# One row for each side's output: 320 columns copied by ScalarE, 256 by VectorE, stored as one run

## The chip, the core and the metric

The kernel runs on one core of one Trainium2 chip. The time is device microseconds of one execution, as the median of several runs. The profile is of one further execution, taken by the hardware profiler; positions inside it are in microseconds from the start of its span.

## What is computed

Two attention layers decode one token each, side A with a window of the last 2048 positions of its cache and side B with all 8192, and their outputs stand side by side in one row of 1152 bf16 values. For each side:

```python
q = (x @ wq).reshape(1, 1, 32, 128)             # x: 1 x 576, wq: 576 x 4096
k, v = k_cache, v_cache                         # 16 heads x 8192 x 128; side A: last 2048 rows
p = softmax(q . k * 128 ** -0.5)                # 32 query heads, two to a kv head
o = p . v                                       # 1 x 4096
return o @ wo                                   # wo: 4096 x 576
```

Everything is bf16 with fp32 accumulation, and the result is `concatenate([a, b])`.

## The kernel before

Every engine's program is a list, filled in order by `op` and `load` and emitted by the class `Prog` with one semaphore for each engine and one for each transfer in flight. An entry waits for the names in its `deps` and then runs in the order of its list.

All loads go through SP's queue into one ring buffer: wq of both sides, then K and V of four units of A and eight units of B, at last wo of A in one piece (`wo0.0`) and wo of B in six pieces (`wo1.0` to `wo1.5`, of 16, 8, 4, 2, 1 and 1 of the 32 slices, after the list `NWO`). The two x rows are loaded by ACT's queue into `xrow`, which lies in one partition.

The unit loop transposes K slabs on VectorE (L367), forms scores on TensorE (L384), takes exponentials on ScalarE (L433), multiplies with V (L460) and folds the result (L476). After the last unit a short chain (L515 to L532) normalizes both sides and leaves `oP`, 128 x 2 x 32.

Then comes the stretch that the change touches, the output projection into the PSUM tile `fb`, which is `qb[0]`. For each side P and each of 32 slices k it does two matmuls (L543) with a stationary operand of one column, `oP[:, P, k]`. They sum into two PSUM rows, 32 x (2P + n), of which row n = 0 holds the first columns of the side's output and row n = 1 the others. So A uses PSUM partitions 0 and 32, B partitions 64 and 96. The matmuls of one piece of wo are one entry, `F0.0` or `F1.0` to `F1.5`, and wait for that piece. When a side's last matmul is done, ScalarE copies row n = 0 to SBUF (`f0.0`, `f1.0`, L551) and VectorE row n = 1 (`f0.1`, `f1.1`, L554), both casting to bf16. SP stores the side when both are done (`out0`, `out1`, L555), and its program ends with a wait for `out1` (L561).

In the profile the copies and the store of both sides have the same lines.

Of the kernel before, what the change touches and what calls it, by code (L numbers as in the profile page):

```python
# [4 lines left out]
BF16 = mybir.dt.bfloat16  # L5
# [3 lines left out]
ACT = mybir.ActivationFunctionType  # L9
# [5 lines left out]
DM = 576  # L15
# [12 lines left out]
ZW = 128 + W0  # L28
ZA = 128 + 24
BIG = 1e30  # L30
RING = 72 * 1024
NSEM = 24
NKT = 3
# [3 lines left out]
class Prog:  # L37
# [9 lines left out]
    def op(self, eng, fn, deps=(), name=None):  # L47
        self.ops[eng].append((fn, tuple(deps), name, None))
        if name is not None:
            assert name not in self.where, name  # L50
            self.where[name] = (eng, len(self.ops[eng]) - 1)

    def load(self, eng, fn, sem, value, deps=(), name=None):
        self.ops[eng].append((fn, tuple(deps), None, sem))
        if name is not None:
            assert name not in self.dma, name
            self.dma[name] = (sem, value)
# [54 lines left out]
def bass_concat_heads__sliding_block_cached__gqa_block_cached__decode_kernel(nc, A_x, A_k_cache, A_v_cache, A_wq, A_wo,  # L112
# [6 lines left out]

    ring = nc.alloc_sbuf_tensor("ring", [128, RING], BF16)  # L120
    ktb = nc.alloc_sbuf_tensor("ktb", [128, NKT * SLAB], BF16)
# [36 lines left out]
    oq = nc.alloc_sbuf_tensor("oq", [128, 2, HQ], BF16)  # L158
    oP = nc.alloc_sbuf_tensor("oP", [128, 2, HQ], BF16)
    warm = nc.alloc_sbuf_tensor("warm", [128, 8], F32)  # L160
    outsb = nc.alloc_sbuf_tensor("outsb", [128, 288], BF16)

    sb = [nc.alloc_psum_tensor("sb%d" % b, [128, 512], F32) for b in range(2)]
    qb = [nc.alloc_psum_tensor("qb%d" % b, [128, 512], F32) for b in range(2)]
# [4 lines left out]
    def view(t, free, offset, dims, parts=128, p0=0):  # L169
        return bass.AP(tensor=t, offset=p0 * free + offset, ap=[[free, parts], *dims])  # L170

    pg = Prog(nc)
    op, load = pg.op, pg.load
    s_x = [nc.alloc_semaphore("s_x%d" % i) for i in range(2)]
    s_ld = [nc.alloc_semaphore("s_ld%d" % i) for i in range(NSEM)]
    s_out = nc.alloc_semaphore("s_out")
# [4 lines left out]
    def place(size, uses, issue, name):  # L181
        if at[0] + size > RING:
            at[0] = 0
        lo, hi = at[0], at[0] + size
        at[0] = hi
        deps = []
        for r in list(live):
            if r[0] < hi and lo < r[1]:
                deps += r[2]
                live.remove(r)  # L190
        n = nload[0]
        nload[0] += 1
        if n >= NSEM:
            deps += uses_of[n - NSEM]
        uses_of.append(list(uses))
        live.append((lo, hi, list(uses)))
        t = ring[:, lo:hi]
        load("sp", lambda e: issue(e, t), s_ld[n % NSEM], 16 * (n // NSEM + 1), deps=deps, name=name)
        return t
# [41 lines left out]
    wo_at = {}  # L241
    for P in range(2):
        k0 = 0
# [6 lines left out]
    def slab(kind, side, u, s):  # L250
# [7 lines left out]
       deps=["id0"], name="ident")  # L258
# [7 lines left out]
    for c in range(2):  # L266
        op("dve", lambda e, c=c: e.tensor_reduce(par[:, c:c + 1], view(identf, 128, c, [[2, 64]]), AX.X, ALU.add),
           deps=["identf"], name="par%d" % c)
# [3 lines left out]
    for P in range(2):  # L272
        op("dve", lambda e, P=P: e.tensor_copy(
            view(xdup, 256, 128 * P, [[2, 64], [1, 2]], parts=1),
            view(xrow, 2 * DM, P * DM + 512, [[1, 64], [0, 2]], parts=1)), deps=["x%d" % P], name="xd%d" % P)
        for k in range(5):
            def mm(e, P=P, k=k):
                if k < 4:
                    lhsT = view(xrow, 2 * DM, P * DM + k, [[4, 128]], parts=1)
                else:  # L280
                    lhsT = xdup[0:1, P, :]
                return e.matmul(banks[2 * P + k // 4][:, (k % 4) * 128:(k % 4 + 1) * 128], lhsT=lhsT,
                                rhs=onesb[0:1, :], start=True, stop=True)
            op("pe", mm, deps=["x%d" % P, "onesb", "xd%d" % P], name="xT%d.%d" % (P, k))
        op("dve", lambda e, P=P: e.tensor_copy(
            xrep[:, P, 0:4, :].rearrange("p k m -> p (k m)"), banks[2 * P][:, :]), deps=["xT%d.3" % P], name="xr%d.0" % P)
        for c in range(2):
            op("dve", lambda e, P=P, c=c: e.tensor_scalar(
                xrep[:, P, 4 + c, :], banks[2 * P + 1][:, 0:128], par[:, c:c + 1], None, ALU.mult),
                deps=["xT%d.4" % P, "par%d" % c], name="xr%d.%d" % (P, 1 + c))  # L290
# [5 lines left out]
    for h in range(2):  # L296
        op("dve", lambda e, h=h: e.tensor_reduce(
            cls[:, 2 * h:2 * h + 2], view(identf, 128, 64 * h, [[1, 2], [32, 2], [2, NB]]), AX.XY, ALU.add),
            deps=["identf"], name="clsB%d" % h)
    op("dve", lambda e: e.tensor_reduce(clsa[:], view(identf, 128, 0, [[1, 8], [8, 16]]), AX.X, ALU.add),  # L300
       deps=["identf"], name="clsa")
    op("dve", lambda e: e.tensor_reduce(sel[:], view(identf, 128, 0, [[1, 32], [32, 4]]), AX.X, ALU.add),
       deps=["identf"], name="sel")
    op("dve", lambda e: e.tensor_copy(mkr[:], view(ident, 128, 0, [[0, 128], [1, 4]], 4)),
       deps=["ident"], name="mkr")
    op("dve", lambda e: e.tensor_scalar(mkl[:], view(ident, 128, 0, [[0, 16], [1, 4], [0, 2]], 4), -1.0, BIG,
                                        ALU.add, ALU.mult), deps=["ident"], name="mkl")
# [4 lines left out]
    for P in range(2):  # L312
        for n in range(8):
            u = 8 * P + n
            bank = banks[u % 4]

            def mm(e, P=P, n=n, bank=bank):
                for k in range(5):
                    if k < 4:
                        lhsT, o = xrep[:, P, k, :], wq_at[P, 0][:, k * w + n * 512:k * w + (n + 1) * 512]  # L320
                    else:
                        lhsT, o = xrep[:, P, 4 + n // 4, :], wq_at[P, 1][:, (n % 4) * 512:(n % 4 + 1) * 512]
                    ins = e.matmul(bank[:, :], lhsT=lhsT, rhs=o, start=(k == 0), stop=(k == 4))  # L323
                return ins
            op("pe", mm, deps=["wq%d.0" % P, "wq%d.1" % P] + XR + (["qe%d" % (u - 4)] if u >= 4 else []),
               name="qmm%d.%d" % (P, n))
            deps = ["qmm%d.%d" % (P, n)] + (["qT%d" % (u - 2)] if u >= 2 else [])
            if n % 2 == 0:
                op("act", lambda e, n=n, bank=bank: e.activation(qsb[:, n % 2, :], bank[:, :], ACT.Copy),  # L329
                   deps=deps, name="qe%d" % u)  # L330
            else:
                op("dve", lambda e, n=n, bank=bank: e.tensor_copy(qsb[:, n % 2, :], bank[:, :]),
                   deps=deps, name="qe%d" % u)
            op("dve", lambda e, n=n: e.transpose(  # L334
                ktb[:, n * 512:(n + 1) * 512].bitcast(I32), qsb[:, n % 2, :].bitcast(I32)),
                deps=["qe%d" % u] + (["z0.%d" % i for i in range(4)] if P else []), name="qT%d" % u)
        srcs = [[512, NP], [64, 2], [1, 2], [128, 2]]
        for b in range(4):
            if P == 1:
# [3 lines left out]
                    deps=["qT%d" % u for u in range(8, 16)] + ["zb0"], name="z1.%d" % b)  # L343
            else:
# [3 lines left out]
                    deps=["qT%d" % u for u in range(8)] + ["za0"], name="z0.%d" % b)  # L348
# [5 lines left out]
    k0 = [sum(nslab[:i]) for i in range(NU)]  # L354
# [129 lines left out]
    for i in range(NU):  # L484
        n = nslab[i + 1] if i + 1 < NU else 0
# [37 lines left out]
       deps=["lsel", "lselA", "nb%d" % last, "mr%d" % last], name="L")  # L523
# [3 lines left out]
        deps=["rl", "O%d" % last], name="on")  # L527
    op("dve", lambda e: e.transpose(oq[:].rearrange("p c k -> p (c k)"), on[:].rearrange("p c k -> p (c k)")),
       deps=["on"], name="oq")
# [5 lines left out]
    fb = qb[0]  # L535
    for P in range(2):
        k0 = 0
        for c, kk in enumerate(NWO[P]):
            def mm(e, P=P, c=c, k0=k0, kk=kk):
                for k in range(kk):  # L540
                    for n in range(2):
                        r = 32 * (2 * P + n)
                        ins = e.matmul(fb[r:r + 1, 0:288], lhsT=oP[:, P, k0 + k:k0 + k + 1],  # L543
                                       rhs=wo_at[P, c][:, k * DM + 288 * n:k * DM + 288 * n + 288],
                                       start=(k0 + k == 0), stop=(k0 + k == HQ - 1))
                return ins
            op("pe", mm, deps=["wo%d.%d" % (P, c), "oP", "exp%d" % (NQ - 2)], name="F%d.%d" % (P, c))
            k0 += kk
        done = "F%d.%d" % (P, len(NWO[P]) - 1)
        r = 64 * P  # L550
        op("act", lambda e, r=r: e.activation(outsb[r:r + 1, :], fb[r:r + 1, 0:288], ACT.Copy),  # L551
           deps=[done], name="f%d.0" % P)
        r = 64 * P + 32
        op("dve", lambda e, r=r: e.tensor_copy(outsb[r:r + 1, :], fb[r:r + 1, 0:288]), deps=[done], name="f%d.1" % P)  # L554
        load("sp", lambda e, P=P: e.dma_start(  # L555
            out[0, 0:1, P * DM:(P + 1) * DM].rearrange("o (n c) -> (o n) c", n=2),
            bass.AP(tensor=outsb, offset=64 * P * 288, ap=[[32 * 288, 2], [1, 288]])),
            s_out, 16 * (P + 1), deps=["f%d.0" % P, "f%d.1" % P], name="out%d" % P)
    op("sp", lambda e: e.nop(), deps=["out1"])

    with nc.Block() as block:  # L561
# [29 lines left out]
```

## Time and profile before

| What | Value |
|---|---|
| median of 3 runs | 248.11 us (248.06 to 248.28) |
| profiled execution | 248.34 us |
| its span | 246.5 us |
| mean granted TensorE clock | 0.827 |
| PE, DVE, ACT busy | 182.0, 146.0, 23.6 us |
| DMA, mean | 418 GB/s over 102.91 MB |
| L543, 128 matmuls of 288 columns | 10.3 us busy |
| L554, 2 copies of 288 columns | 0.9 us busy, 458 ns each |
| L551, 2 copies of 288 columns | 400 ns each |

A line of the profile names a source line, an engine, an operation and `output<-inputs` by tile, then how often and for how long it ran, and for idle time of the engine before it who ended it. Spans of matmuls that run side by side are merged, so a busy time can be shorter than the number times the duration. PE is TensorE's multiplication, DVE VectorE, ACT ScalarE, SP the engine that issues transfers; an engine's name with q stands for its queue.

### The profile page before, as it was taken

How to read it: one execution, taken by the hardware profiler on the slowest of the kernel's cores; microseconds unless marked ns; L12 is line 12 of the kernel's file. 1: busy time of each engine (PE TensorE's matmuls, PEld its weight loads, DVE VectorE, ACT ScalarE, POOL GpSimd, SP SyncE). 2: the span in 40 equal slices, each digit the busy share in tenths (PEclk: the TensorE clock that was granted, in tenths of full speed). 3: DMA queues.
4: the chain of work that ended last, by engine and by line, in shares of the span. 5: the costliest groups of instructions: out<-in, count | busy, mean ns of one | idle time of the engine just before them, and what ended most of it. 6: DMA issues, size and time to landing. Idle time of an engine off the chain costs nothing.

```text
span 246.5 us, 2421 instructions
## 1 busy us (share of the span) xinstructions
PE 182.0 (74%) x1009; PEld 75.6 (31%) x1009; DVE 146.0 (59%) x224; ACT 23.6 (10%) x48; POOL 1.8 (1%) x12
## 2 busy tenths in 40 slices
PE   1169958778868599489769858949929949985694
PEld 0024423223332152152142233224205205231461
DVE  3466976786869569169349448547646836922200
ACT  2002210101201010010001001001001001001000
POOL 2000000000000000000000000000000000000000
PEclk9999997799999958957955976965985895796579
DMA  6999999999999999999999999999999999999992
GB/s 261 425 479 402 433 425 419 425 425 463 431 417 431 425 425 431 423 441 452 441 431 433 425 431 425 425 423 427 431 425 431 449 431 431 431 437 431 401 406 103
DMA packets 5062, 102.91 MB, mean 418 GB/s; under 512 B 566, under 2 KB 828, under 8 KB 1340
## 3 DMA queue, kind: packets, MB, share of 16 engines
q1 hardware_dynamic: 5048, 102.77, 97.6%
q8 instruction: 8, 0.13, 0.2%
q14 instruction: 2, 0.02, 0.0%
q10 hardware_dynamic: 4, 0.00, 0.0%
HBM read 102.76 MB, written 0.00 MB: 417 GB/s over the span
## 4 chain that ended last, share of the span: by engine, by line
DMA 56%; PE 20%; DVE 19%; issue 1%; SPq 1%; ACT 0%; DVEq 0%
DMA ring<-in_B_k_cache_dram 41%; DVE ktb L367 15%; DMA ring<-in_B_wo_dram 10%; DMA ring<-in_A_wq_dram 5%; PE sb L323 4%; PE sb L384 4%; PE qb L384 4%; PE qb L323 3%; PE ob L476 3%; DVE pts L445 2%; PE mb L424 1%; SPq L246 1%; DVE pta L441 0%; PE qb L376 0%; DVE nb L430 0%
## 5 line engine op out<-in xcount | busy, mean ns | idle before, releaser
L367 DVE STREAM_TRANSPOSE ktb<-ring 128x1024 int32<-128x1024 int32 x80 | 95.1, 1221 | 16.7 <-DMA ring<-in_B_k_cache_dram 15.8
L384 PE MATMUL sb<-ktb,zb 128*128 128x512 bf16 x256 | 84.4, 468 | 27.3 <-DVE ktb L367 27.3
L384 PEld LDWEIGHTS sb<-ktb,zb 128*128 128x128 bf16 x256 | 23.2, 109 | 77.6 <-DVE ktb L367 45.3
L460 PE MATMUL vb<-ring,pts 128*16 128x512 bf16 x256 | 20.6, 412 | 2.6 <-DVE pts L445 2.6
L384 PE MATMUL qb<-ktb,za 128*128 128x512 bf16 x64 | 19.1, 436 | 2.9 <-DVE ktb L367 2.9
L476 PEld LDWEIGHTS ob<-sel,xo 128*128 128x128 f32 x96 | 19.5, 285 | 4.9 <-issue 2.2
L399 DVE TENSOR_REDUCE mx<-sb 128x1 f32<-128x512 f32 x8 | 5.5, 692 | 21.9 <-PE sb L384 21.9
L476 PE MATMUL ob<-sel,xo 128*128 128x4 f32 (+1 forms) x96 | 17.7, 309 | 0.7 <-ACT xo L467 0.7
L467 ACT ACTIVATE xo<-vb 128x512 f32<-128x512 f32 x12 | 7.2, 597 | 89.2 <-PE vb L460 89.2
L323 PE MATMUL sb<-ring,xrep 128*128 128x512 bf16 x40 | 11.4, 441 | 5.3 <-DMA ring<-in_A_wq_dram 5.3
L430 DVE COPY nb<-mb 128x1 f32<-128x1 f32 x12 | 1.9, 159 | 21.1 <-PE mb L424 21.1
L433 ACT ACTIVATE psb<-sb,nb 128x512 bf16<-128x512 f32 x8 | 5.5, 687 | 65.3 <-DVE nb L430 65.3
L445 DVE STREAM_TRANSPOSE pts<-psb 64x512 bf16<-64x512 bf16 x16 | 11.0, 688 | 1.0 <-ACT psb L433 0.8
L543 PE MATMUL qb<-ring,oP 128*1 128x288 bf16 x128 | 10.3, 328 | 1.2 <-DMA ring<-in_B_wo_dram 0.6
L384 PEld LDWEIGHTS qb<-ktb,za 128*128 128x128 bf16 x64 | 5.7, 106 | 13.4 <-DVE ktb L367 6.4
L401 PE MATMUL mb<-identf,mx 128*1 128x128 f32 x24 | 4.6, 271 | 7.1 <-DVE mx L399 7.1
L334 DVE STREAM_TRANSPOSE ktb<-qsb 128x256 int32<-128x256 int32 x16 | 7.1, 446 | 4.4 <-ACT qsb L329 4.0
L323 PE MATMUL qb<-ring,xrep 128*128 128x512 bf16 x40 | 9.4, 381 | 0.0
L460 PEld LDWEIGHTS vb<-ring,pts 128*16 128x16 bf16 x256 | 4.1, 90 | 16.9 <-issue 15.6
L323 PEld LDWEIGHTS sb<-ring,xrep 128*128 128x128 bf16 x40 | 4.2, 109 | 11.6 <-issue 8.2
L543 PEld LDWEIGHTS qb<-ring,oP 128*1 128x1 bf16 x128 | 5.6, 94 | 5.8 <-DMA ring<-in_B_wo_dram 2.2
L554 DVE CAST outsb<-qb 1x288 bf16<-1x288 f32 x2 | 0.9, 458 | 10.8 <-PE qb L543 10.8
(73 smaller groups left out, 71.9 us busy)
## 6 DMA issues: line engine op xcount, KB each, us to landing
ring<-in_B_k_cache_dram SPq DMA_DIRECT2D x8, 4096.0 KB, 25.3
ring<-in_B_v_cache_dram SPq DMA_DIRECT2D x8, 4096.0 KB, 33.0
ring<-in_A_k_cache_dram SPq DMA_DIRECT2D x4, 2048.0 KB, 30.9
ring<-in_A_v_cache_dram SPq DMA_DIRECT2D x4, 2048.0 KB, 26.4
ring<-in_A_wo_dram SPq DMA_DIRECT2D x1, 4608.0 KB, 16.4
ring<-in_A_wq_dram SPq DMA_DIRECT2D x1, 4096.0 KB, 12.1
ring<-in_B_wq_dram SPq DMA_DIRECT2D x1, 4096.0 KB, 22.2
ring<-in_B_wo_dram SPq DMA_DIRECT2D x1, 2304.0 KB, 21.5
```

What stands on the lines that cost most here:

```text
L323: ins = e.matmul(bank[:, :], lhsT=lhsT, rhs=o, start=(k == 0), stop=(k == 4))
L334: op("dve", lambda e, n=n: e.transpose(ktb[:, n * 512:(n + 1) * 512].bitcast(I32), qsb[:, n % 2, :].bitcast(I32)), deps=["qe%d" % u] + ([" ...
L367: op("dve", lambda e: e.transpose(kt.bitcast(I32), src.bitcast(I32)), deps=["K%d" % i] + (["S%d" % (k - NKT)] if k >= NKT else Z), name="T ...
L384: ins = e.matmul(bank[:, :], lhsT=lhsT, rhs=view(ktb, KT, (k % NKT) * SLAB + 64 * c + v, [[128, 16], [2, 32]]), start=(side == "B" and s = ...
L399: op("dve", lambda e: e.tensor_reduce(mx[:, 0:1], sbank[i][:, :], AX.X, ALU.max), deps=["S%d" % (k0[i] + nslab[i] - 1)] + (["mT%d" % (i - ...
L401: op("pe", lambda e: e.matmul(mb[0:1, 0:128], lhsT=mx[:, 0:1], rhs=identf[:, :], start=True, stop=True), deps=["max%d" % i] + was, name="m ...
L433: op("act", lambda e: e.activation(psb[:, :], sbank[i][:, :], ACT.Exp, bias=nb[:, c:c + 1], scale=SCALE, accum_out=acc), deps=["nb%d" % i, ...
L445: op("dve", lambda e, h=h: e.transpose(view(pts, 1024, 2 * h, [[4, 16], [64, 16], [1, 2]], 64, 64 * h), psb[64 * h:64 * h + 64, :]), deps= ...
L460: ins = e.matmul(vbank[i][32 * j:32 * j + n, :], lhsT=lhsT, rhs=src[:, 512 * j:512 * j + 512], start=(s == 0), stop=(s == nslab[i] - 1))
L467: op("act", lambda e: e.activation(xo[:, c, :], vbank[i][:, :], ACT.Copy), deps=["V%d.%d" % (i, nslab[i] - 1)] + (["O%d" % (i - 1)] if i e ...
L476: ins = e.matmul(ob[:, at:at + w], lhsT=xo[:, c, 128 * t:128 * t + 128], rhs=sel[:, w * t:w * t + w], start=(t == 0), stop=(t == 3))
L543: ins = e.matmul(fb[r:r + 1, 0:288], lhsT=oP[:, P, k0 + k:k0 + k + 1], rhs=wo_at[P, c][:, k * DM + 288 * n:k * DM + 288 * n + 288], start= ...
```

## The change

The matmuls split a side's 576 columns at `N0 = 320` instead of 288, so that row n = 0 has 320 columns and row n = 1 has 256. `outsb` becomes one row of one partition for both sides. ScalarE copies the 320 columns and VectorE the 256, each to its place in that row, and a side's store moves one contiguous run of 576 values instead of two runs of 288 from two partitions.

```diff
+N0 = 320
...
-    outsb = nc.alloc_sbuf_tensor("outsb", [128, 288], BF16)
+    outsb = nc.alloc_sbuf_tensor("outsb", [1, 2 * DM], BF16)
...
                     for n in range(2):
-                        r = 32 * (2 * P + n)
-                        ins = e.matmul(fb[r:r + 1, 0:288], lhsT=oP[:, P, k0 + k:k0 + k + 1],
-                                       rhs=wo_at[P, c][:, k * DM + 288 * n:k * DM + 288 * n + 288],
+                        r, lo, hi = 32 * (2 * P + n), n * N0, N0 + n * (DM - N0)
+                        ins = e.matmul(fb[r:r + 1, 0:hi - lo], lhsT=oP[:, P, k0 + k:k0 + k + 1],
+                                       rhs=wo_at[P, c][:, k * DM + lo:k * DM + hi],
                                        start=(k0 + k == 0), stop=(k0 + k == HQ - 1))
...
-        r = 64 * P
-        op("act", lambda e, r=r: e.activation(outsb[r:r + 1, :], fb[r:r + 1, 0:288], ACT.Copy),
+        r, lo = 64 * P, P * DM
+        op("act", lambda e, r=r, lo=lo: e.activation(outsb[0:1, lo:lo + N0], fb[r:r + 1, 0:N0], ACT.Copy),
            deps=[done], name="f%d.0" % P)
-        r = 64 * P + 32
-        op("dve", lambda e, r=r: e.tensor_copy(outsb[r:r + 1, :], fb[r:r + 1, 0:288]), deps=[done], name="f%d.1" % P)
-        load("sp", lambda e, P=P: e.dma_start(
-            out[0, 0:1, P * DM:(P + 1) * DM].rearrange("o (n c) -> (o n) c", n=2),
-            bass.AP(tensor=outsb, offset=64 * P * 288, ap=[[32 * 288, 2], [1, 288]])),
-            s_out, 16 * (P + 1), deps=["f%d.0" % P, "f%d.1" % P], name="out%d" % P)
+        op("dve", lambda e, r=r, lo=lo: e.tensor_copy(outsb[0:1, lo + N0:lo + DM], fb[r + 32:r + 33, 0:DM - N0]),
+           deps=[done], name="f%d.1" % P)
+        load("sp", lambda e, lo=lo: e.dma_start(out[0, 0:1, lo:lo + DM], outsb[0:1, lo:lo + DM]),
+             s_out, 16 * (P + 1), deps=["f%d.0" % P, "f%d.1" % P], name="out%d" % P)
```

## The prediction

> **What bounds the kernel now.** I read the page first, then the chain of waits over the last 30 us, the timeline of the same stretch, the answers for the tile outsb and for the matmul line L543, the granted clock by stretch, and the DMA traffic in short windows. The page's queue line says that the queue which carries all the loads is busy almost the whole span:
>
> ```profile
> q1 hardware_dynamic: 5048, 102.77, 97.6%
> ```
>
> The chain of waits (start, length, what) shows how the span ends:
>
> ```profile
> 218.84 24.77 DMA ring<-in_B_wo_dram
> 243.62 0.04 issue
> 243.66 0.31 PE qb L543 x2
> 243.97 0.02 issue
> 243.99 0.47 DVE outsb L554
> ```
>
> The last 144 KB piece of B's wo lands at 243.62; one pair of matmuls, one copy and the store follow. All that the change touches is in or beside this tail. The profiled execution took 248.34 us with a span of 246.5, so 1.84 lie outside the span; the median of the three runs is 248.11, 0.23 lower. I make the sum as a difference in the profiled execution and take it off the median.
>
> The timeline of the output projection (start, length from first start to last end, then idle time before and its releaser):
>
> ```profile
> 232.87 7.58 PE L543 MATMUL qb<-ring,oP 128*1 128x288 bf16 x96 [0.41 <-DVE oP L532]
> 240.80 1.14 PE L543 MATMUL qb<-ring,oP 128*1 128x288 bf16 x16 [0.35 <-DMA ring<-in_B_wo_dram]
> 242.20 1.74 PE L543 MATMUL qb<-ring,oP 128*1 128x288 bf16 x16 [0.26 <-DMA ring<-in_B_wo_dram]
> ```
>
> A's 64 matmuls and the first 32 of B run without a stop; then PE waits for each piece of wo. So PE is ahead of the DMA by the time the last pieces come, and the amount by which it is ahead is what the change spends. The granted clock, PEclk, in the stretches of L543:
>
> ```profile
> core 0: us, PE busy (x) PEld busy (x), PEclk, DMA share, GB/s
> 233.10:236.60 3.50, 3.50 (x32) 1.90 (x30) 0.50 0.98 416
> 237.30:238.25 0.95, 0.95 (x20) 0.66 (x16) 1.00 0.94 393
> ```
>
> Most of A's half runs at half clock, the rest at full clock. Three lines for the tile outsb (min/median/max ns) and one of SP's waits (us, times, longest) price what follows the last matmul:
>
> ```profile
> L551 ACT ACTIVATE outsb<-qb x2: 399/400/401, 239.0 to 244.0; 1x288 bf16<-1x288 f32 x2
> L554 DVE CAST outsb<-qb x2: 451/458/465, 239.0 to 244.0; 1x288 bf16<-1x288 f32 x2
> L555 SPq DMA_DIRECT2D out_dram<-outsb x2: 543/588/632, 239.5 to 244.5; - x2
> ```
>
> ```profile
> SPq L561 <- DMA out_dram<-outsb: 1.0, 1, 1.0
> ```
>
> Nothing follows A's store out0 but the wait for B's: A's copies and store lie four microseconds before the end and count only through the queues that they share.
>
> **The copies.** On the path is the later of two concurrent copies, DVE's, 465 ns from 243.99. The 512-column copies of the same kind give the price of a column:
>
> ```profile
> L332 DVE CAST qsb<-sb 128x512 bf16<-128x512 f32 x4 | 2.7, 682 | 1.1 <-PE sb L323 1.1
> L329 ACT ACTIVATE qsb<-sb 128x512 bf16<-128x512 f32 x4 | 2.4, 597 | 18.4 <-PE sb L323 18.4
> ```
>
> DVE: (682 - 458) / 224 = 1.0 ns a column, so 256 columns take 465 - 32 = 433. ACT: (597 - 400) / 224 = 0.88, so 320 take 401 + 28 = 429. They then end within 4 ns of each other and SP is released 32 ns earlier: -0.03. Both now write partition 0, from PSUM rows 64 and 96; no copy of this trace moves its row to another partition, and no two engines write one partition together. The copies of the trace cost what their columns say, whatever their partitions, so I take nothing for that; the bounds are -0.03 (gain kept) and +0.40 (the two copies run one after the other: 433 + 429 - 465).
>
> **The matmuls.** Their number stays 128, but a pair is 320 + 256 columns instead of 288 + 288. The two of a pair start 2 to 4 ns apart in the trace's records and each lasts 283 ns or more, while successive pairs start 240 ns apart at half clock and 122.5 at full clock: 288 columns, not 576, set the rhythm. The wider half will set it: 240 x 320 / 288 = 267, and 122.5 + 32 x 0.42 = 136 (0.42 ns being the 120 ns of 288 columns at full clock). The Trainium skill says it too (TensorEngine Tiling (Array Packing), Key Properties: different tiles can execute matmuls in parallel), so by page and row alike an uneven split is the worse one, by 11% of this stretch.
>
> Where that goes, step by step. In the records A's first pair starts at 232.87, its second at 233.06, and full clock comes at about 237.03. At 267 ns pair 17 starts at 237.05, and fifteen more at 136 put pair 32 at 239.08; before it was at 238.68: 0.40 late. B's first 16 pairs began before A's last (238.32) and now begin at about 238.70, the last at 240.74 instead of 240.16. The next piece lands at 240.80, so of the 0.35 that PE waited there nothing is left and its eight pairs start 0.08 late, at 240.88; the last starts at 241.83, with the next free start at 241.96. The following piece lands only at 242.20: the delay is gone. Its four pairs take 0.54 to 242.75, the next piece lands at 242.93, two pairs take 0.27 to 243.20, the next lands at 243.30, one pair, and the last lands at 243.62. Hidden by these waits, the cost is nothing; without them it would be the whole 0.4 and the rhythm of each later pair. Slack left is 0.24 + 0.18 + 0.10 + 0.22 = 0.74 us. In the last pair the wider matmul ends 32 x 0.42 = 13 ns later, the narrower 13 earlier: +0.01 if the copies wait for the wider one.
>
> **The store.** The DMA moves one run of 1152 bytes instead of two of 576. Around the last store the traffic (245.6 to 245.8) shows two data packets and two semaphore packets; A's x, a load of one row of 1152 bytes, shows one of each (1.4 to 1.75):
>
> ```profile
> DMA packets 4, 0.00 MB, mean 6 GB/s; under 512 B 2, under 2 KB 4, under 8 KB 4
> ```
>
> ```profile
> DMA packets 2, 0.00 MB, mean 3 GB/s; under 512 B 1, under 2 KB 2, under 8 KB 2
> ```
>
> So I expect one packet. The copying itself is nothing: 1152-byte packets take 51 ns and the pair of 576 (29 each) spanned 48. The issue is the unknown. The nearest rows are the stores (543, 632) and the two one-row issues on ACT's queue:
>
> ```profile
> 0.73 0.51 ACTq L203 DMA_DIRECT2D xrow<-in_A_x_dram  x1
> 1.28 0.21 ACTq L203 DMA_DIRECT2D xrow<-in_B_x_dram  x1
> ```
>
> The price of the new issue lies between 212 and 543 or a little more: -0.33 to +0.09 (the 632 of A's store). From issue to first packet x took 0.90 us, the last store 1.17: -0.27 by that count. I take -0.10, nearer to SP's own row, because x is a load on another queue. The 1.0 us that SP then waits I leave.
>
> There is a rule of the Trainium skill against the change: DMA: Bandwidth & Descriptors (Why a DMA increments its semaphore by 16) says that software can split a contiguous single row so that it spreads over 16 engines, and its Specifications that writes under 512 B are read, modified and written. By that the store would be 16 pieces of 72 bytes; x, the same shape, was not split here.
>
> **Sum.** -0.03 (copies) + 0.01 (last pair) - 0.10 (store) = -0.12: 248.34 to 248.22, and the median 248.11 to about 248.0. That is 0.05%; about 0.2%, 0.5 us, is what a measurement of this kernel can tell from no change.
>
> **Rivals.** *Faster: the store in one packet saves far more.* The issue falls to ACT's 212 (-0.33), the copies give 0.03, and SP's 1.0 us wait shrinks because one engine reports instead of two. For: everything between the last copy's end (244.46) and the span's end (246.47) is one store, 2.0 us. Against: two packets were only 19 ns apart, so the second costs little; the issue of other transfers of 16 engines on SP takes 328 to 443, not less. It passes 0.2% when the wait gives 0.14 or more beside the issue; time 247.4 (0.36 of the wait gone too) to 247.75 (none).
>
> *Slower: PE becomes the bound of the tail.* Each microsecond by which full clock comes later delays the projection by about half (267 against 136 ns a pair). After 0.74 / 0.49 = 1.5 us, that is at 238.5 instead of 237.03, the slack is spent and each further microsecond costs 0.49. Before, the slack was about 1.55 us, good for full clock as late as 240.2, so steady times of before do not show that the clock's step is steady. To pass 0.2% it must come at about 239.8 (0.49 x 1.3 - 0.12 = 0.5); at 240.5 the time is 248.0 + 0.98 = 249.0. (TensorE: Matmul & The Clock Gate, Part 1, gives the step a free-running window of 3.4 us; one such shift would cost 0.9; no view here shows the shift between runs.)
>
> *Slower by much: uneven pairs don't overlap.* Pairs then take 480 and 240 ns: ten are done by 237.03, 22 of A end at 242.3, B's 31 first pairs at 249.8 instead of 243.66: some 6 us, 254. Nothing here runs tiles of unequal width together.
>
> *Not one row after all.* Split in 16 pieces, the store's issue would be near the 328 to 443 of other 16-engine issues, the landing that of the slowest engine; -0.2 to +0.3, around 248.1.
>
> **How the numbers follow.** Forecast 0.62, all within 0.2%; one step dearer than its bounds 0.01, within. Faster rival 0.20, of which 0.15 past the bound. Sixteen pieces 0.05, of which 0.01 slower. Late PE 0.10, of which 0.08 slower. No overlap 0.02, slower. So faster 0.15, slower 0.11, same 0.74. The bounds of the forecast's own costs make 248.11 - 0.03 - 0.33 = 247.75 at the low end and, with copies one after the other and an issue like A's, 248.11 + 0.40 + 0.01 + 0.09 = 248.6 at the high end. The range goes down to 247.6, into the faster rival, and ends at 248.6, where late PE has used 0.6.
>
> **What would show it.** Right: pairs of L543 136 ns apart at full clock and 267 at half; PE's wait before the first 240.8 piece gone, that before 242.2 still there; L554 near 433, L551 near 429; one data packet at the end, an issue of L555 under 543. Wrong: no wait on in_B_wo_dram before the last pairs (PE bound), more than two packets around the store, or L551 and L554 longer than their columns.

## The result, and the profile after

| | before | after |
|---|---|---|
| median | 248.28 us (248.06 to 248.61) | 247.85 us (247.66 to 248.06) |
| profiled execution | 248.34 us | 247.88 us |
| its span | 246.5 us | 246.1 us |

Each median is of 21 executions in one series; the ratio is 0.9981, with a 95% interval of 0.9975 to 0.9988. The kernel is 0.43 to 0.47 us faster. That is clear of noise, inside the range, on the side that was forecast and still within 0.2%, but over three times the 0.12 us of the sum. The prediction took 0.2% as the least that can be told from no change; with 21 executions of each kernel the interval reaches 0.07% to either side.

The chain of waits of after ends as before did, on the last piece of wo, one pair of matmuls and a copy:

```profile
218.68 25.03 DMA ring<-in_B_wo_dram
243.71 0.04 issue
243.75 0.32 PE qb L544 x2
244.07 0.02 issue
244.09 0.43 ACT outsb L552
```

The copy that ends last is now ACT's, of 0.43 instead of 0.47, and the lines of the source have moved down by one. So the last piece landed no earlier (243.71 against 243.62) and the span is nevertheless 0.38 shorter: the time was gained behind the last copy. The answer for outsb in after has the copies at 320 and 256 columns and, in the last line, the store's issue:

```profile
L552 ACT ACTIVATE outsb<-qb x2: 426/428/429, 238.7 to 244.1; 1x320 bf16<-1x320 f32 x2
L554 DVE CAST outsb<-qb x2: 416/421/426, 238.7 to 244.1; 1x256 bf16<-1x256 f32 x2
L556 SPq DMA_DIRECT2D out_dram<-outsb x2: 249/286/322, 239.2 to 244.6; - x2
```

DVE's copy fell by 39 ns from 465. The issue of B's store fell from 543 to 249 ns, that of A's from 632 to 322. The timeline gives the last issue's place, and the traffic of the window 245.2 to 245.5 what it sent:

```profile
244.59 0.25 SPq L556 DMA_DIRECT2D out_dram<-outsb  x1
```

```profile
DMA packets 2, 0.00 MB, mean 4 GB/s; under 512 B 1, under 2 KB 2, under 8 KB 2
```

One data packet of 1152 bytes and one semaphore packet, instead of two and two. From the records of the two traces, step by step to the end of the span, in us:

| Step | before | after | difference |
|---|---|---|---|
| start of the last pair, set by the last piece of wo | 243.66 | 243.75 | +0.09 |
| to the copies' start | 0.33 | 0.34 | +0.01 |
| to the end of the later copy | 0.467 | 0.429 | -0.04 |
| to the start of the issue | 0.07 | 0.07 | 0 |
| to the first data packet | 1.175 | 0.732 | -0.44 |
| to SP's going on | 0.388 | 0.394 | +0.01 |
| to the end of the span | 0.38 | 0.38 | 0 |
| sum, before rounding | | | -0.38 |

The store's start is the whole gain: 0.29 of it inside the issue, 0.15 between the issue's end and the first packet (0.632 before, 0.483 after).

### The profile page after: what moved, and what is told of

It reads as the page before. It is cut to its first block, busy times and chain, and to the rows that moved or that the text cites. A ratio compares the mean times of both kernels' runs of the same rounds, so it can differ in the third digit from the quotient of the medians.

```text
span 246.1 us, 2421 instructions
## 1 busy us (share of the span) xinstructions
PE 182.6 (74%) x1009; PEld 75.8 (31%) x1009; DVE 146.0 (59%) x224; ACT 23.6 (10%) x48; POOL 1.8 (1%) x12
## 4 chain that ended last, share of the span: by engine, by line
DMA 57%; PE 22%; DVE 16%; issue 2%; SPq 1%; ACT 0%; DVEq 0%
DMA ring<-in_B_k_cache_dram 31%; DVE ktb L368 13%; DMA ring<-in_B_v_cache_dram 10%; DMA ring<-in_B_wo_dram 10%; PE qb L385 6%; DMA ring<-in_A_wq_dram 5%; PE sb L324 4%; PE sb L385 4%; PE qb L324 3%; PE ob L477 2%; DVE pts L446 2%; PE mb L425 1%; SPq L247 1%; PE qb L377 1%; PE vb L461 0%
## 5 line engine op out<-in xcount | busy, mean ns | idle before, releaser
L385 PE MATMUL sb<-ktb,zb 128*128 128x512 bf16 x256 | 83.1, 462 | 25.4 <-DVE ktb L368 25.4
L461 PE MATMUL vb<-ring,pts 128*16 128x512 bf16 x256 | 21.1, 420 | 3.9 <-DVE pts L446 2.6
L385 PE MATMUL qb<-ktb,za 128*128 128x512 bf16 x64 | 21.5, 488 | 1.5 <-DVE ktb L368 1.5
L477 PEld LDWEIGHTS ob<-sel,xo 128*128 128x128 f32 x96 | 18.5, 272 | 4.5 <-issue 1.6
L477 PE MATMUL ob<-sel,xo 128*128 128x4 f32 (+1 forms) x96 | 16.9, 301 | 0.7 <-ACT xo L468 0.7
L324 PE MATMUL sb<-ring,xrep 128*128 128x512 bf16 x40 | 10.6, 418 | 6.6 <-DMA ring<-in_A_wq_dram 5.7
L544 PE MATMUL qb<-ring,oP 128*1 128x320 bf16 (+1 forms) x128 | 10.8, 318 | 1.4 <-DMA ring<-in_A_wo_dram 0.7
L385 PEld LDWEIGHTS qb<-ktb,za 128*128 128x128 bf16 x64 | 6.4, 115 | 13.8 <-issue 7.0
L544 PEld LDWEIGHTS qb<-ring,oP 128*1 128x1 bf16 x128 | 6.6, 90 | 5.5 <-DMA ring<-in_B_wo_dram 2.2
L554 DVE CAST outsb<-qb 1x256 bf16<-1x256 f32 x2 | 0.8, 421 | 11.5 <-PE qb L544 11.5
```

Source lines behind the costliest of these rows:

```text
L385: ins = e.matmul(bank[:, :], lhsT=lhsT, rhs=view(ktb, KT, (k % NKT) * SLAB + 64 * c + v, [[128, 16], [2, 32]]), start=(side == "B" and s = ...
L461: ins = e.matmul(vbank[i][32 * j:32 * j + n, :], lhsT=lhsT, rhs=src[:, 512 * j:512 * j + 512], start=(s == 0), stop=(s == nslab[i] - 1))
L477: ins = e.matmul(ob[:, at:at + w], lhsT=xo[:, c, 128 * t:128 * t + 128], rhs=sel[:, w * t:w * t + w], start=(t == 0), stop=(t == 3))
L544: ins = e.matmul(fb[r:r + 1, 0:hi - lo], lhsT=oP[:, P, k0 + k:k0 + k + 1], rhs=wo_at[P, c][:, k * DM + lo:k * DM + hi], start=(k0 + k == 0 ...
```

## The experiments

Theory: a store of one contiguous run is issued and started 0.44 us sooner than one of several runs, and nothing else of the change can be measured. Rivals: that the gain comes from the widths, from the source lying in one partition, or from the number of engines. The difference of each kernel is shown against after unless it says otherwise. "First packet" is counted from the start of the last store's issue, "landing" from the first packet to SP's going on. The reference point for a ratio is before, run on the same chip.

| Kernel | runs, engines | issue, ns | first packet, ns | landing, ns | ratio to before (95%) |
|---|---|---|---|---|---|
| before | 2, 2 | 543 | 1175 | 388 | 1 |
| after | 1, 1 | 249 | 732 | 394 | 0.9981 (0.9975 to 0.9988) |
| store alone | 1, 1 | 249 | 734 | 395 | 0.9982 (0.9973 to 0.9991) |
| two runs | 2, 2 | 620 | 1257 | 387 | 1.0003 (0.9994 to 1.0012) |
| four runs | 4, 4 | 630 | 1264 | 421 | 1.0006 (0.9997 to 1.0014) |
| sixteen runs | 16, 16 | 544 | 1201 | 498 | 1.0004 (0.9995 to 1.0013) |
| 23 runs, one engine | 23, 1 | 617 | 1245 | 635 | 1.0008 (0.9999 to 1.0018) |
| ACT's queue | 1, 1 | 224 | 713 | 393 | 0.9983 (0.9974 to 0.9991) |
| two queues (SP, ACT) | 1 and 1 | 249, 224 | 750, 713 | 623 | 0.9995 (0.9986 to 1.0003) |

The trace does not name the engines; I count one for each semaphore packet beside the data packets. That fits the data packets' starts in the records: of the sixteen runs' packets the first four start within 3 ns, while those of the 23 runs follow one another, 4 to 10 ns apart.

**The store alone.**

```diff
-N0 = 320
+N0 = 288
```

> The change with the columns split 288/288 again: only the one-row, one-run store is left of it. Theory 'one run': the gain is the store's issue and its start; SP's issue of the last store takes about 250 ns instead of 543, the data packet starts about 0.73 us after the issue instead of 1.17, and the time is 0.40 us below before, ratio 0.998. The copies are DVE's 465 and ACT's 400 again, which gives 0.04 back against the change. Rival 'widths': the gain is in the copies and the projection; then the time is that of before, ratio 1.000.

Measured: 247.85 us. Its answer for outsb:

```profile
L554 DVE CAST outsb<-qb x2: 449/454/459, 238.1 to 244.1; 1x288 bf16<-1x288 f32 x2
L556 SPq DMA_DIRECT2D out_dram<-outsb x2: 249/286/323, 238.6 to 244.6; - x2
```

The copy is long again, the issue short, and the time is that of after. The one-run store is the whole measurable gain; the rival "widths" falls. The 30 ns between the copies (459 and 429) are too little for a ratio that is known to 0.0009, or 0.22 us.

**Two, four and sixteen runs from one partition.** The row has a gap of 32 bytes between runs (`RL` = 576 / `NR` values in a run, `RP` = `RL` + 16), and the copies write around the gaps. For two runs:

```diff
-N0 = 320
+N0 = 288
+NR = 2
+RL = DM // NR
+RP = RL + 16
...
-e.dma_start(out[0, 0:1, lo:lo + DM], outsb[0:1, lo:lo + DM])
+e.dma_start(out[0, 0:1, lo:lo + DM].rearrange("o (n c) -> o n c", n=NR),
+            view(outsb, 2 * NR * RP, lo // DM * NR * RP, [[RP, NR], [1, RL]], 1))
```

> As the store alone (288/288, one partition), but with 32 bytes between the two halves of a side in the row, so that the store moves two runs of 576 bytes out of the same partition. Theory 'one run': issue near 543 ns, first packet near 1.17 us after it, time as before, ratio 1.000. Rival 'one partition': what counts is that the source lies in one partition; then issue near 250 ns and ratio 0.998.

> As the two runs, but four runs of 288 bytes from one partition. If each run or engine has its price, the issue is above 543 ns and the time 0.1 to 0.5 us above that of two runs; if any split store pays one fixed price over a single run, it is as with two runs, ratio 1.000. If fewer increments that SP has to make up for itself make it cheaper (12 instead of 14), the issue is a little under 543 ns.

> As the two runs, but sixteen runs of 72 bytes from one partition. If the price is one per run, this is the dearest of all, over 1 us above the single run. If the issue of a transfer on all sixteen engines is cheap, like the wo loads' 328 to 443 ns, the issue is there and the time lies between the change and before, 247.9 to 248.2, unless writes of 72 bytes land late: then the time from packet to SP's going on is well over the 0.39 us of before and after, by 0.1 us or more.

Measured: 248.33, 248.41 and 248.41 us. The issue lines from their answers for outsb, in that order:

```profile
L561 SPq DMA_DIRECT2D out_dram<-outsb x2: 620/678/737, 239.2 to 244.4; - x2
```

```profile
L561 SPq DMA_DIRECT2D out_dram<-outsb x2: 630/688/747, 238.9 to 244.3; - x2
```

```profile
L561 SPq DMA_DIRECT2D out_dram<-outsb x2: 544/574/604, 239.2 to 244.7; - x2
```

Two runs out of one partition lose the whole gain, so "one partition" falls; they even start 0.08 later than the two runs out of two partitions of before (1257 against 1175). From two runs to sixteen the start stays near 1.2 us: no price per run. The expectations of a price per run or per engine and of a cheap issue on sixteen engines were both wrong; that of one fixed price held. What did grow is the landing, by 0.10 to 0.11 us at sixteen runs. That is the spread of the packets: the last data packet starts 0.136 us after the first, and from it to SP's going on it takes 0.362 us, no longer than the 0.369 of before. The traffic of its window (245.8 to 246.2) has sixteen data and sixteen semaphore packets:

```profile
DMA packets 32, 0.00 MB, mean 3 GB/s; under 512 B 32, under 2 KB 32, under 8 KB 32
```

**Many runs on one engine.** This one separates the number of runs from the number of engines, which were equal so far.

```diff
-N0 = 320
+N0 = 288
...
-e.dma_start(out[0, 0:1, lo:lo + DM], outsb[0:1, lo:lo + DM])
+e.dma_start(bass.AP(tensor=out.tensor, offset=out.offset + lo, ap=[[2 * DM, 1], [25, 23], [1, 24]]),
+            view(outsb, 2 * DM, lo, [[25, 23], [1, 24]], 1))
```

> The store alone (288/288, one partition), but as 23 runs of 48 bytes, each 24 of 25 columns, in the row and in the output alike; every 25th column and the last column of each side are left out of the output. 23 has no divisor up to 16, so one engine should take all of it, with one semaphore packet. If the number of engines sets the price, SP's issue of the last store is near 250 ns and the first packet 0.73 us after it; the packets then follow at 10 to 20 ns, 0.3 us in all, and the time is 0.1 below before, 248.1. If it is the number of runs, the issue is near 540 to 630 ns and the first packet 1.2 us after it, and the time is 0.3 above before, 248.55.

Measured: 248.46 us. The traffic (245.5 to 246.5) shows 23 data packets and one semaphore packet, and the issue is long:

```profile
DMA packets 24, 0.00 MB, mean 1 GB/s; under 512 B 24, under 2 KB 24, under 8 KB 24
```

```profile
L556 SPq DMA_DIRECT2D out_dram<-outsb x2: 617/680/743, 238.9 to 244.3; - x2
```

One engine, but the start of a store of several runs: the engines don't set the price. It is a single run against more than one. Why more than one costs 0.44 us the trace does not show: 0.29 of it is inside the issue and 0.15 between the issue and the first packet. The landing of this kernel is the longest, 0.635: its packets take 0.162 from the first start to the last, and from the last one 0.473 pass, about 0.1 more than in the other kernels with one queue; this 0.1 is not explained.

**Other queues for the single run.**

```diff
-load("sp", lambda e, lo=lo: e.dma_start(out[0, 0:1, lo:lo + DM], outsb[0:1, lo:lo + DM]),
+load("act" if P else "sp", lambda e, lo=lo: e.dma_start(out[0, 0:1, lo:lo + DM], outsb[0:1, lo:lo + DM]),
```

> The change, but B's store issued from ACT's queue after both copies; SP only waits for it. If the issue and start depend on the one run alone, ACT's issue takes 210 to 510 ns as for x and the first packet starts 0.73 us after it: time as the change, 247.85. If ACT's queue starts later, as x's 0.90 us, the time is 0.17 above the change, 248.0.

Measured: 247.79 us, and its timeline:

```profile
244.43 0.22 ACTq L556 DMA_DIRECT2D out_dram<-outsb  x1
```

The same short issue and start on the other queue, so x's second issue, 212 ns, was the right row for this store. In the next one, ACT stores its 320 columns after its own copy and SP the 256 after VectorE's:

```diff
+        if P == 0:
...
+        else:
+            load("act", lambda e, lo=lo: e.dma_start(out[0, 0:1, lo:lo + N0], outsb[0:1, lo:lo + N0]),
+                 s_x[0], 32, deps=["f1.0"], name="out1a")
+            load("sp", lambda e, lo=lo: e.dma_start(out[0, 0:1, lo + N0:lo + DM], outsb[0:1, lo + N0:lo + DM]),
+                 s_out, 32, deps=["f1.1"], name="out1")
+    op("sp", lambda e: e.nop(), deps=["out1a", "out1"])
```

> The change, but B's 320 columns stored from ACT's queue as soon as ACT's copy is done and the 256 from SP's as soon as VectorE's is done: two single runs at once instead of one. If a single run is cheap wherever it is issued, the time is that of the change, 247.85, less at most 0.05 for the wait that is gone; if two transfers in flight disturb each other's issue or start, 0.1 to 0.4 above, up to that of before, 248.25.

Measured: 248.07 us. Issues and start are short for both:

```profile
244.14 0.25 SPq L562 DMA_DIRECT2D out_dram<-outsb  x1
244.15 0.22 ACTq L560 DMA_DIRECT2D out_dram<-outsb  x1
```

But the landing, from the first of the two data packets, is 0.623 instead of 0.394, and most of the gain is lost. In the records each transfer counts up a semaphore of its own. ACT's has landed 0.367 us after its packet, as quickly as a single store (0.377 in after). SP's packet starts 31 ns after ACT's and has landed 0.520 us after its own start, some 0.14 late. SP waits for its own transfer first and goes on 0.055 after that wait has passed. Together these are 0.031 + 0.143 + 0.055 = 0.229, all of the difference. Why the later of the two transfers lands late is not settled. It was expected that issue or start would suffer; neither did.

**Wider splits.** These test the other half of the prediction, that the waits for wo hide the slower pairs until the slack is spent.

```diff
-N0 = 320
+N0 = 384
```

> The change with the columns split 384/192. Theory 'the rhythm of the wider half is hidden by the waits for wo as long as the slack lasts': pairs of L544 take 320 ns at half clock and 162 at full; with full clock at about 236.2 the slack is overspent by some 0.3 us, the last pair starts near 244.05 without a wait on wo, ACT's copy takes 485 ns, and the time is 0.3 to 0.5 us above the change, about 248.2. Rival 'PE is never on the path': only copy and last matmul count, 0.08 above the change, 247.9. Rival 'the extra columns count in full': 17 pairs of 53 ns and 47 of 27 more, 2.2 us, 250.0.

```diff
-N0 = 320
+N0 = 448
```

> The same with 448/128. Theory 'hidden until the slack is spent': pairs take 373 ns at half clock and 189 at full, PE ends the tail, the last pair starts near 245.6 instead of 243.75, ACT's copy takes 541 ns; 2.0 us above the change, 249.9 (0.5 more or less for each microsecond by which full clock comes later or earlier than 236.2). Rival 'never on the path': 0.17 above, 248.0. Rival 'in full': 4.4 us above, 252.2.

Measured: 248.72 us (247.80 to 249.29 over 12 executions), ratio 1.0019 (1.0010 to 1.0027), and 250.15 us (249.49 to 250.69 over 4), ratio 1.0073 (1.0056 to 1.0090). The chain of waits of 384/192 has no wo of B left in it. From A's wo on it is PE to the end:

```profile
232.46 12.51 PE qb L544 x65
244.97 0.02 issue
244.99 0.48 ACT outsb L552
```

PE has become the bound, as the walk through the pieces said. "Never on the path" (247.9 and 248.0) and "in full" (250.0 and 252.2) both fall. The medians are 0.5 and 0.25 over the expected values; full clock came later than the 236.2 that they assumed. The granted clock (PEclk) in the projection of the two profiled executions:

```profile
233.00:237.70 4.70, 4.70 (x34) 1.92 (x31) 0.50 0.96 408
237.80:244.60 6.80, 6.80 (x92) 3.69 (x90) 1.00 0.62 243
```

```profile
233.00:237.70 4.70, 4.70 (x28) 1.67 (x26) 0.50 0.97 410
237.80:246.50 8.70, 8.70 (x96) 3.83 (x94) 1.00 0.48 188
```

At 237.7 instead of 236.2 the rule of 0.49 us for each microsecond makes 0.74 more: 248.94 and 250.64, against 248.79 and 250.43 of these executions. A second profile of the same 384/192 kernel tests the rule itself.

> The same kernel as the split 384/192, for another place of the clock's step. Theory 'full clock decides when the slack is spent': the last pair's start moves by half of what full clock's start moves against 237.7 of the other profile, down to 243.7 where the DMA takes over; each 1 us earlier gives 0.5 us less. If the spread of that kernel's times, 247.8 to 249.3, has another cause, the last pair's start does not follow the step.

Measured: 248.00 us in one execution, with full clock 2.0 us earlier:

```profile
233.00:235.70 2.70, 2.70 (x22) 1.14 (x18) 0.50 1.00 427
235.80:243.70 7.90, 7.90 (x104) 4.36 (x102) 1.00 0.79 315
```

In the records the step is at 235.76 instead of 237.72, and the last pair starts at 243.74 instead of 244.62: 0.88 for 1.96 us, or 0.45 for each, where 0.49 was expected. The projection itself began 0.13 later, which at half clock is worth 0.07; with it the rule gives 0.48. So between these two profiles the time follows the clock's step. That the spread of all twelve times has the same cause is likely but not shown: one of the twelve was profiled, and the slowest, 249.29, would need a step near 238.8 by this rule, later than the latest that any profile shows (237.88).

## Why the prediction was right, and what it mis-sized

**Right: what bounds the end.** The last piece of wo sets the end before and after. The copies moved as priced: 429 for ACT (429 expected), 426 for DVE (433), and the last pair's +0.01 was measured. Writing one partition from two engines and moving a row to another partition cost nothing that shows: the 288-column copy into partition 0 took 459 ns in the store alone and 465 to its own partition.

**Right: the slower pairs are hidden.** In the records of after the 320-column matmuls follow each other at 267 ns at half clock and 136 at full, as worked out; the 256-column ones run ahead of them, by two at most. The wait before the piece at 240.8 was forecast to vanish, and in the profile of after it did not:

```profile
240.89 1.25 PE L544 MATMUL qb<-ring,oP 128*1 128x320 bf16 x16 [0.46 <-DMA ring<-in_B_wo_dram]
```

There full clock came at 235.78, 1.25 us before the 237.03 of the sum, and the projection began 0.28 earlier. In the kernel with ACT's queue, which has the same matmuls, it came at 237.44: there B's second piece follows its first without a wait, all 128 matmuls stand as one unbroken stretch in the timeline (the later waits leave gaps of at most 0.05 us in it, too short to split the line), and the end is still set by the last piece of wo, with the slack not spent:

```profile
232.44 11.44 PE L544 MATMUL qb<-ring,oP 128*1 128x320 bf16 x128 [2.33 <-DMA ring<-in_A_wo_dram]
```

**Mis-sized: the store.** The step "I take -0.10, nearer to SP's own row" failed; the term measured -0.44. The sum's own bound of -0.36 (-0.03 and -0.33) is passed by the measured -0.43; that 247.85 still lies above the 247.75 of that bound is luck, since before's median is 248.28 in the series of the result and was 248.11 in that of the prediction. Two choices made the term small. I took the store's own row of two runs as nearest because queue and direction agreed, and the row with the same shape, x with one run, as farther. The shape was what mattered: 212 on ACT was close to the measured 249 on SP and 224 on ACT. And I bounded the term by the issue alone, at -0.33, while the start of the first packet also moved, by 0.15 after the issue's end; the count by first packet, -0.27, was spoiled by x's first issue, which took 511 ns at the start of the program. The argument against the faster rival, that two packets lie only 19 ns apart, looked at the packets, and the price lies ahead of the first. That rival had the right place and nearly the right issue (-0.33 against -0.29); its other part, SP's wait, did get shorter, from 1.0 to 0.9 in the views (1.02 to 0.88 in the records):

```profile
SPq L560 <- DMA out_dram<-outsb: 0.9, 1, 0.9
```

But the reason given, that one engine reports instead of two, was wrong: packet to going on stayed at 0.39, and the 0.14 comes from the packet that starts sooner after the issue. The forecast had left this wait unchanged.

**Not one row after all** did not happen: one data packet. In the sixteen-run kernel, which does what this rival feared, the time was 248.41 where before had 248.25, as this rival's price allowed. The Trainium skill's rule that software can split a contiguous single row (DMA: Bandwidth & Descriptors, Why a DMA increments its semaphore by 16) did not bear on this store. In the sixteen-run kernel writes of 72 bytes cost nothing that shows beyond the spread of their packets; whether they are read and modified first no run shows.

**Late PE** did not decide for 320/256: the latest step in any profile is 237.88, before the 238.5 at which the sum had the slack spent. 384/192 shows it 64 columns on.

## What to carry to other kernels

A last store that is one contiguous run on both sides started 0.4 to 0.5 us sooner here than any with two to 23 runs, whatever the number of engines, and was as quick from ACT's queue as from SP's; where a kernel ends on a small store, gather it into one row first and don't split it over two queues, which cost 0.22 us here. Price a transfer by the row with its number of runs before the row with its queue, and count to its first packet, not to the end of its issue. Work hidden behind a stream of loads has a slack that can be walked through piece by piece; check it against the latest place of the clock's step, since one profile shows only one place.

## What the runs showed of the hardware that was not expected

- A store's start has two levels: 713 to 750 ns from issue to first packet with one run, 1175 to 1264 with 2, 4, 16 or 23 runs, on one, two, four or sixteen engines.
- Of two stores of one run each, in flight together from two queues, the one whose packet started first landed after 0.367 us, as a single one does; the other, 31 ns behind it, took 0.520.
- Two matmuls of unequal width that sum into different PSUM rows keep their own rhythms: at half clock, in after, the 320-column ones start every 267 ns and the 256-column ones every 213, so the narrower row runs ahead, but in A's half of all six profiles with uneven halves by two matmuls at most; from there it starts about 6 ns after the wider one and keeps its rhythm (every 320 ns at half clock in 384/192).
- The step to full clock in the tail falls at another place in each execution: from 235.30 to 237.88 in the twelve profiles of these kernels (237.03 in that of before, 235.78 in that of after).
